# A spectral and MLP layer on one core: copies of x, an unread maximum and the written order of the first stage

## The chip, the cores and the metric

The kernel runs on one core of a Trainium2 chip. A time is the device time of one execution in microseconds (us). The core has a matrix engine (PE, with its weight loads PEld), a vector engine (DVE), an activation engine (ACT), a general engine (POOL) and SyncE (SP), which issues most transfers. Each engine works through its own instructions in the order in which they were written, and waits for another engine only where a semaphore says so. A transfer (DMA) runs beside the engines once it is issued. SBUF is the memory on the chip (the kernel's one large buffer there is called `arena`), PSUM holds the results of matmuls, and DRAM is the memory behind both.

## The reference

x has 2048 rows (tokens) of 576 numbers. It is normalised along each row to xn, and three things are added:

```
xn = (x - mean(x)) / sqrt(var(x) + 1e-5)
A  = Cr @ (xn @ Dr.T) - Ci @ (xn @ Di.T)     # Cr, Ci: 2048 x 2048; Dr, Di: 576 x 576
B  = relu(xn @ w1) @ w2                      # w1: 576 x 4608, w2: 4608 x 576
out = x + A + B
```

## The kernel before

**Number format.** The inputs are float32. Each operand of a matmul is written as a sum of two float16 numbers, a high part (made by ACT) and a low part (what is left, made by DVE or POOL), and a product takes three matmuls: high by high, high by low, low by high. Large products are formed from seven products of quarter blocks instead of eight, with sums and differences of the blocks formed by DVE.

**Stages.** Tokens are taken in 16 tiles of 128 rows, and four tiles make a group of 512. The columns of w1 are taken in 9 blocks. A step (block, group) computes a part of xn @ w1 and relu, and the second matmul of the step before. Sums of the second layer are collected in a DRAM buffer `spill`, which starts as a copy of x (`copy_x`) and to which every step adds by an accumulating transfer that POOL issues (`mlp2_out`, L665). Behind the steps come xn times the two small transform matrices, and then the product with the 2048 x 2048 matrices, which makes most of the rest.

**The first stage** covers about the first 80 us: the normalisation of all tiles and block 0 for the groups 0 to 2. Its order is written out by hand as a list of some 380 items; `pinned` runs them one by one and ties each instruction behind the one written before it on the same engine (PE, ACT, DVE, POOL, SP), so the list fixes the order on every engine. It fixes nothing between two engines; there only data and buffers decide. The items are:

- `counts`, `moments`, `stats`: mean, variance and factor of a tile or of a group of tiles (DVE, L271 to L299; the first step of `stats` is a square root on ACT, L289).
- `normal`, `high_x`, `low_x`, `again`: xn in float32, its high part, the low part in two pieces (piece 0 has 64 columns, piece 1 has 512), and a copy of the last 128 columns. The engine (V for DVE, A for ACT, GP for POOL) is an argument.
- `transposes` and `copies`: a tile is transposed by PE and copied out of PSUM by ACT (tiles 0 to 3). `transposes_dma` (L336): the same by a transfer that SP issues (tiles 4 to 15).
- `max_w1`, `sum_w2`, `steps_of`: scale factors of the weights; `steps_of` takes one small step, in turns on PE and DVE. `hi1`, `lo1`, `hi2`, `lo2`, `diff2`: the weights' parts and differences.
- `fill n`: n matmuls on zeros whose result nobody reads (PE, L914).
- `tile_by` (one tile) and `products` (a group of 512 rows): xn @ w1 on PE (L380). `outputs`: relu and the parts of its result (ACT and DVE, L431 to L441).
- `mlp2_mm` (PE, L643) and `mlp2_out` (ACT L658 or DVE L662, and POOL L665): the second layer, seven products, their evictions and the transfers that add to `spill`.
- `library` (L928): the maximum over partitions of a constant, on POOL, which nobody reads. It is the first instruction of that kind on POOL; the next ones scale block 1's weights (L168).
- `copy_x g` (L879): four transfers from x in DRAM to the four parts of `spill` for group g, 288 KB each, issued by SP.
- `work`: the next step of the preparation of block 1 (its loads L154 and L142, maxima L162, and the split of its weights, L232 on ACT and L235 on DVE).

Four staging buffers hold the normalised tiles; tile t uses buffer t % 4, so tile 12 takes the buffer that tile 8 had, once its transpose has landed. Block 1's split weights are written to the same memory, so the split waits for the transposes of tiles 12 to 14. The first matmuls of group 3 (the first thing behind the list) need the transposes of tiles 12 to 15.

The loads stand ahead of the list: on SP, the 16 tiles of x, the weights w1 of block 0 between the first tiles, and w2 behind tile 7.

```
def copy_x(g):
    for row, col in itertools.product(range(2), range(2)):
        ...
        with behind("td"):
            nc.sync.dma_start(spill[g, row, col], src.rearrange("(c p) e -> p c e", p=P))
```

`behind("td")` ties the copy behind the last `transposes_dma` written so far, if there is one.

Of the kernel before, what the change touches and what calls it, by code (L numbers as in the profile page):

```python
# [32 lines left out]
KM = 4  # L33
# [22 lines left out]
def kernel(  # L56
# [894 lines left out]
    for f, *a in (  # L951
        (counts, 0),
        (moments, 0),
        (stats, 0),
        (max_w1, 0, 0),
        (stats, 0),
        (fill, 50),
        (fill, 25),
        (stats, 0),
        (stats, 0),  # L960
        (stats, 0),
        (stats, 0),
        (max_w1, 0, 1),
        (steps_of, wa),
        (counts, 1),
        (high_x, 0),
        (normal, 0, A),
        (steps_of, wa),
        (fill, 4),
        (moments, 1),  # L970
        (stats, 1),
        (counts, 2),
        (stats, 1),
        (transposes, 0, *H),
        (fill, 10),
        (steps_of, wa),
        (steps_of, wa),
        (low_x, 0, 0, V),
        (copies, 0, 0, KM),
        (stats, 1),  # L980
        (steps_of, wa),
        (moments, 2),
        (hi1, 0),
        (stats, 1),
        (low_x, 0, 1, GP),
        (fill, 4),
        (steps_of, wa),
        (fill, 11),
        (transposes, 0, KM, NKX),
        (stats, 1),  # L990
        (stats, 1),
        (max_w1, 0, 2),
        (counts, 3),
        (high_x, 1),
        (moments, 3),
        (normal, 1, A),
        (max_w1, 0, 3),
        (stats, 2),
        (stats, 2),
        (counts, 5),  # L1000
        (stats, 2),
        (fill, 3),
        (low_x, 1, 0, V),
        (hi1, 1),
        (fill, 9),
        (tile_by, 0, (0,), XH[0], True, False),
        (stats, 2),
        (fill, 31),
        (low_x, 1, 1, GP),
        (transposes, 0, *L[1:-1]),  # L1010
        (transposes, 1, *H),
        (fill, 7),
        (transposes, 1, *L[1:-1]),
        (transposes, 1, KM, NKX),
        (copies, 0, KM, NKX + 1),
        (fill, 11),
        (copies, 1, 0, KM),
        (lo1, 0),
        (stats, 2),
        (stats, 2),  # L1020
        (tile_by, 0, (0,), XL, False, False),
        (copies, 1, KM, NKX + 1),
        (steps_of, wb),
        (lo1, 1),
        (steps_of, wb),
        (fill, 9),
        (tile_by, 0, (0,), XH[1], False, True),
        (normal, 2, V),
        (high_x, 2),
        (steps_of, wb),  # L1030
        (steps_of, wb),
        (tile_by, 0, (1,)),
        (low_x, 2, 0, V),
        (steps_of, wb),
        (counts, 4),
        (tile_by, 1, (0, 1), XH[0] + XH[1], True, False),
        (high_x, 3),
        (low_x, 2, 1, GP),
        (normal, 3, V),
        (low_x, 3, 1, GP),  # L1040
        (counts, 6),
        (sum_w2, 0, 0),
        (hi1, 2),
        (transposes, 2, *H),
        (moments, 5),
        (transposes, 2, *L[1:-1]),
        (counts, 7),
        (moments, 6),
        (moments, 4),
        (moments, 7),  # L1050
        (transposes, 2, KM, NKX),
        (copies, 2, 0, NKX + 1),
        (transposes, 3, *H),
        (tile_by, 1, (0, 1), XL, False, True),
        (low_x, 3, 0, GP),
        (lo1, 2),
        (transposes, 3, *L[1:-1]),
        (transposes, 3, KM, NKX),
        (tile_by, 2, (1,)),
        (tile_by, 2, (0,)),  # L1060
        (hi1, 3),
        (stats, 4),
        (stats, 4),
        (tile_by, 0, (2,)),
        (stats, 4),
        (stats, 4),
        (stats, 4),
        (stats, 4),
        (copies, 3, 0, NKX + 1),
        (lo1, 3),  # L1070
        (tile_by, 3, (0,)),
        (high_x, 4),
        (again, 4, GP),
        (tile_by, 2, (2,)),
        (normal, 4, V),
        (counts, 8),
        (normal, 5, A),
        (tile_by, 2, (3,)),
        (counts, 9),
        (counts, 11),  # L1080
        (outputs, 0, 0, "r"),
        (high_x, 5),
        (high_x, 6),
        (moments, 11),
        (tile_by, 1, (2,)),
        (moments, 9),
        (sum_w2, 0, 1),
        (normal, 6, V),
        (counts, 10),
        (tile_by, 3, (1,)),  # L1090
        (normal, 7, A),
        (tile_by, 3, (2,)),
        (steps_of, wb),
        (steps_of, wc),
        (moments, 10),
        (low_x, 4, 0, GP),
        (moments, 8),
        (low_x, 4, 1, GP),
        (stats, 8),
        (counts, 14),  # L1100
        (low_x, 5, 1, GP),
        (outputs, 0, 0, "hA"),
        (tile_by, 0, (3,)),
        (steps_of, wc),
        (stats, 8),
        (high_x, 7),
        (outputs, 0, 0, "hB"),
        (transposes_dma, 4),
        (low_x, 5, 0, GP),
        (low_x, 6, 0, GP),  # L1110
        (again, 6, GP),
        (tile_by, 1, (3,)),
        (stats, 8),
        (stats, 8),
        (again, 7, A),
        (again, 5, GP),
        (stats, 8),
        (stats, 8),
        (low_x, 6, 1, GP),
        (counts, 15),  # L1120
        (normal, 8, V),
        (high_x, 8),
        (normal, 10, A),
        (low_x, 7, 0, GP),
        (steps_of, wc),
        (tile_by, 3, (3,)),
        (transposes_dma, 5),
        (outputs, 0, 0, "s3"),
        (tile_by, 4, (0, 1)),
        (steps_of, wc),  # L1130
        (steps_of, wc),
        (tile_by, 5, (0, 1)),
        (outputs, 0, 1, "r"),
# [3 lines left out]
        (low_x, 7, 1, GP),  # L1137
        (outputs, 0, 0, "lA"),
        (low_x, 8, 0, V),
        (steps_of, wc),  # L1140
        (high_x, 9),
        (again, 8, A),
        (low_x, 8, 1, GP),
        (outputs, 0, 1, "s3"),
        (counts, 13),
        (transposes_dma, 6),
        (outputs, 0, 1, "s2"),
        (steps_of, wc),
        (low_x, 9, 1, GP),
        (high_x, 10),  # L1150
        (outputs, 0, 0, "s2"),
        (transposes_dma, 7),
        (high_x, 11),
        (outputs, 0, 1, "s1"),
        (steps_of, wc),
        (tile_by, 6, (0, 1)),
        (normal, 11, A),
        (tile_by, 7, (0, 1)),
        (outputs, 0, 1, "s4"),
        (outputs, 0, 0, "s4"),  # L1160
        (again, 9, GP),
        (again, 10, A),
        (low_x, 10, 1, GP),
        (outputs, 0, 1, "hA"),
        (steps_of, wc),
        (products, 1, 2),
        (outputs, 0, 1, "hB"),
        (outputs, 0, 0, "lB"),
        (hi2, 0, 0),
        (low_x, 9, 0, V),  # L1170
        (outputs, 0, 0, "s1"),
        (outputs, 0, 1, "lA"),
        (hi2, 1, 0),
        (products, 1, 3),
        (counts, 12),
        (lo2, 0, 0),
        (moments, 15),
        (lo2, 1, 0),
        (outputs, 1, 0, "r"),
        (outputs, 0, 0, "hS"),  # L1180
        (diff2, 0),
        (diff2, 1),
        (outputs, 0, 0, "lS"),
        (outputs, 1, 0, "s3"),
        (low_x, 10, 0, GP),
        (transposes_dma, 8),
        (diff2, 2),
        (low_x, 11, 0, GP),
        (outputs, 1, 0, "hB"),
        (hi2, 0, 1),  # L1190
        (moments, 14),
        (mlp2_mm, 0, 0, 0),
        (outputs, 1, 0, "s2"),
        (outputs, 0, 1, "hS"),
        (outputs, 1, 0, "hA"),
        (diff2, 3),
        (moments, 12),
        (transposes_dma, 9),
        (outputs, 1, 0, "lA"),
        (moments, 13),  # L1200
        (again, 11, GP),
        (outputs, 0, 1, "lB"),
        (hi2, 0, 2),
        (stats, 12),
        (transposes_dma, 10),
        (lo2, 0, 2),
        (low_x, 11, 1, GP),
        (outputs, 1, 0, "lB"),
# [6 lines left out]
        (outputs, 1, 0, "s1"),  # L1215
        (hi2, 1, 2),
        (mlp2_out, 0, 0, 0),
        (outputs, 0, 1, "lS"),
        (stats, 12),
        (outputs, 1, 1, "r"),  # L1220
        (lo2, 1, 2),
        (copy_x, 1),
        (hi2, 1, 1),
        (outputs, 1, 1, "hB"),
        (outputs, 1, 0, "hS"),
        (mlp2_mm, 0, 0, 1),
        (stats, 12),
        (mlp2_mm, 0, 0, 2),
        (outputs, 2, 0, "r"),
        (mlp2_out, 0, 0, 1),  # L1230
        (library,),
        (lo2, 1, 1),
        (mlp2_out, 0, 0, 2),
        (outputs, 1, 0, "lS"),
        (outputs, 1, 1, "s1"),
        (outputs, 2, 0, "s3"),
        (work, 0),
        (stats, 12),
        (mlp2_mm, 0, 0, 3),
        (stats, 12),  # L1240
        (mlp2_out, 0, 0, 3),
        (mlp2_mm, 0, 0, 4),
        (stats, 12),
        (normal, 14, A),
        (mlp2_out, 0, 0, 4),
        (outputs, 1, 1, "hA"),
        (outputs, 1, 1, "s3"),
        (mlp2_mm, 0, 0, 5),
        (work, 0),
        (outputs, 1, 1, "s2"),  # L1250
        (mlp2_mm, 0, 0, 6),
        (high_x, 15),
        (outputs, 1, 1, "s4"),
        (outputs, 1, 1, "lA"),
        (outputs, 2, 0, "s2"),
        (high_x, 13),
        (products, 2, 2),
        (high_x, 14),
        (work, 0),
        (mlp2_out, 0, 0, 5),  # L1260
        (outputs, 2, 0, "s1"),
        (normal, 15, A),
        (outputs, 1, 1, "lB"),
        (outputs, 2, 0, "hA"),
        (mlp2_out, 0, 0, 6),
        (outputs, 1, 1, "hS"),
        (again, 15, A),
        (again, 14, A),
        (outputs, 2, 0, "s4"),
        (mlp2_mm, 0, 1, 0),  # L1270
        (low_x, 15, 0, V),
        (high_x, 12),
        (mlp2_mm, 0, 1, 1),
        (normal, 12, V),
        (mlp2_out, 0, 1, 0),
        (products, 2, 3),
        (normal, 13, A),
        (outputs, 1, 1, "lS"),
        (low_x, 15, 1, V),
        (work, 0),  # L1280
        (mlp2_mm, 0, 1, 2),
        (low_x, 14, 0, V),
# [658 lines left out]
```

## Time and profile before

| | us |
|---|---|
| median of 3 runs | 1221.6 |
| lowest, highest | 1218.69, 1224.0 |
| the profiled execution | 1222.13 |
| its span, first to last instruction | 1220.4 |
| PE busy in the span | 1210.1 |
| DVE busy | 1007.9 |
| ACT busy | 724.4 |
| POOL busy | 161.0 |

Times inside the trace count from the span's first instruction. A row of a timeline gives the start, the time taken, engine, line, operation, what is written <- what is read, the shape and the number of instructions merged into it; in square brackets stands the idle time of the engine before it and what ended that. A row of the waits gives the waiting engine and line, what it waited for, the us in total, how often, and the longest.

### The profile page before, as it was taken

How to read it: one execution, taken by the hardware profiler on the slowest of the kernel's cores; microseconds unless marked ns; L12 is line 12 of the kernel's file. 1: busy time of each engine (PE TensorE's matmuls, PEld its weight loads, DVE VectorE, ACT ScalarE, POOL GpSimd, SP SyncE). 2: the span in 40 equal slices, each digit the busy share in tenths (PEclk: the TensorE clock that was granted, in tenths of full speed). 3: DMA queues.
4: the chain of work that ended last, by engine and by line, in shares of the span. 5: the costliest groups of instructions: out<-in, count | busy, mean ns of one | idle time of the engine just before them, and what ended most of it. 6: DMA issues, size and time to landing. Idle time of an engine off the chain costs nothing.

```text
span 1220.4 us, 24658 instructions
## 1 busy us (share of the span) xinstructions
PE 1210.1 (99%) x10233; PEld 958.5 (79%) x10233; DVE 1007.9 (83%) x1642; ACT 724.4 (59%) x1082; POOL 161.0 (13%) x199
## 2 busy tenths in 40 slices
PE   9989999999999999999999999999999999999998
PEld 8656567888888888888888888877777777777776
DVE  9988999887797788788877977678898978787875
ACT  7755565876676766757767766555644433433332
POOL 3231211111121211111121211100000000000000
PEclk9999999999999999999999999999999999999999
DMA  7895554867667675667576676520165254534320
GB/s 259 197 189 127 99 96 107 168 135 164 155 128 169 131 185 128 136 156 156 127 172 159 120 166 155 98 31 1 62 215 169 72 185 138 177 109 146 101 89 20
DMA packets 84064, 164.66 MB, mean 135 GB/s; under 512 B 22640, under 2 KB 43632, under 8 KB 83952
## 3 DMA queue, kind: packets, MB, share of 16 engines
q1 hardware_dynamic: 61168, 120.61, 31.1%
q0 software_dynamic: 22784, 42.48, 24.7%
q8 instruction: 80, 1.31, 0.4%
q14 instruction: 32, 0.26, 0.1%
HBM read 110.76 MB, written 53.08 MB: 134 GB/s over the span
## 4 chain that ended last, share of the span: by engine, by line
PE 94%; DMA 2%; DVE 2%; ACT 1%; issue 0%; SPq 0%; DVEq 0%; ACTq 0%
PE p L643 29%; PE p L1841 27%; PE bank L548 22%; PE p L380 7%; PE U L1630 4%; PE W L1630 2%; PE bank L567 1%; PE V L1630 1%; DMA arena<-in_x_dram 1%; DMA arena<-in_cim_dram 1%; DMA arena<-arena 1%; DVE arena L235 1%; DMA arena<-in_cre_dram 0%; ACT arena L232 0%; PE U L1646 0%
## 5 line engine op out<-in xcount | busy, mean ns | idle before, releaser
L643 PE MATMUL p<-arena 128*128 128x288 f16 x3024 | 398.6, 286 | 1.8 <-DVE arena L662 1.8
L643 PEld LDWEIGHTS <-arena 128*128 128x128 f16 x3024 | 295.9, 98 | 77.3 <-issue 2.2
L1841 PE MATMUL p<-arena 128*128 128x288 f16 x2688 | 329.4, 286 | 0.0
L1841 PEld LDWEIGHTS <-arena 128*128 128x128 f16 x2688 | 263.0, 98 | 66.3
L548 PE MATMUL bank<-arena 128*128 128x256 f16 x2580 | 304.8, 273 | 0.0
L548 PEld LDWEIGHTS <-arena 128*128 128x128 f16 x2580 | 250.2, 98 | 37.4 <-issue 5.9
L232 ACT ACTIVATE arena<-arena,sc_c 128x1024 f16<-128x1024 f32 x112 | 128.5, 1149 | 189.8 <-PE p L1841 137.8
L665 POOL DMA_DIRECT2D spill<-arena x144 | 128.7, 912 | 547.2 <-DVE arena L662 454.0
L235 DVE SCALAR_TENSOR_TENSOR arena<-arena,sc_c 128x1024 f16<-128x1024 f32 x112 | 143.3, 1280 | 29.4 <-ACT arena L232 26.4
L658 ACT ACTIVATE arena<-p,c_ub 128x576 f32<-128x576 f32 x144 | 105.9, 735 | 45.5 <-PE p L643 40.7
L235 DVE SCALAR_TENSOR_TENSOR arena<-arena,c_sw 128x640 f16<-128x640 f32 (+2 forms) x118 | 96.5, 848 | 32.5 <-ACT arena L232 30.6
L662 DVE SCALAR_TENSOR_TENSOR arena<-p,c_ub,arena 128x576 f32<-128x576 f32 x108 | 87.8, 813 | 22.2 <-PE p L643 19.6
L380 PE MATMUL p<-arena 128*128 128x128 f16 (+1 forms) x680 | 100.0, 303 | 3.1 <-issue 2.8
L576 DVE TENSOR_TENSOR arena<-bank,arena 128x512 f32<-128x512 f32 x84 | 57.7, 687 | 54.2 <-PE bank L548 53.2
L573 ACT ACTIVATE arena<-bank 128x512 f32<-128x512 f32 x112 | 66.5, 594 | 52.0 <-PE bank L548 51.9
L232 ACT ACTIVATE arena<-arena,c_sw 128x640 f16<-128x640 f32 (+2 forms) x118 | 89.3, 793 | 9.4 <-issue 4.5
L1630 PEld LDWEIGHTS <-arena 128*128 128x128 f16 x738 | 71.6, 98 | 19.7 <-issue 1.9
L380 PEld LDWEIGHTS <-arena 128*128 128x128 f16 x680 | 52.4, 98 | 43.3 <-issue 7.4
L579 ACT ACTIVATE arena<-arena 128x512 f16<-128x512 f32 x84 | 52.9, 630 | 52.5 <-DVE arena L576 51.6
L1849 DVE SCALAR_TENSOR_TENSOR arena<-p,us_c,arena 128x288 f32<-128x288 f32 x112 | 57.4, 513 | 27.0 <-PE p L1841 26.6
L1491 ACT ACTIVATE arena<-arena 128x1024 f32<-128x1024 f32 x64 | 67.0, 1047 | 7.6 <-DMA arena<-in_cim_dram 6.0
L589 DVE TENSOR_TENSOR arena<-arena 128x1024 f16<-128x1024 f32 x56 | 68.1, 1217 | 0.3 <-ACT arena L585 0.3
(134 smaller groups left out, 1050.4 us busy)
## 6 DMA issues: line engine op xcount, KB each, us to landing
spill<-arena POOLq DMA_DIRECT2D x144, 288.0 KB, 5.1
arena<-in_cre_dram SPq DMA_DIRECT2D x64, 512.0 KB, 4.6
arena<-in_cim_dram SPq DMA_DIRECT2D x64, 512.0 KB, 4.8
arena<-in_w_dram SPq DMA_DIRECT2D x17, 640.0 KB, 5.8
arena<-in_w_dram SPq DMA_DIRECT2D x18, 576.0 KB, 4.0
arena<-spill SPq DMA_DIRECT2D x40, 144.0 KB, 2.2
arena<-in_x_dram SPq DMA_DIRECT2D x16, 288.0 KB, 7.0
spill<-in_x_dram SPq DMA_DIRECT2D x16, 288.0 KB, 6.9
```

The lines of the kernel that those rows point to most:

```text
L232: nc.scalar.activation(hi, src, AF.Copy, scale=s)
L235: nc.vector.scalar_tensor_tensor(lo, src, s, hi, ALU.mult, ALU.subtract)
L380: order["m1"] = nc.tensor.matmul(ps[:, cols], w1s[b, i // 2][:, hl, i % 2 * KT + k], xT[g][:, kx, cols], start=(start and n == 0), stop=(s ...
L548: nc.tensor.matmul(ps[:, i], l, r, start=first and i == m == 0, stop=m == len(todo) - 1, skip_group_check=not first or i > 0,)
L589: order["lo"] = nc.vector.tensor_tensor(lo, stage[:, 1 + 2 * i :][:, :2], hi, ALU.subtract).ins
L643: order["pe"] = nc.tensor.matmul(ps[:, c], h[:, x, qa, c * P : (c + 1) * P], w[:, y, qb], start=first and i == 0 and j == 0, stop=i == NQ ...
L658: freed(nc.scalar.activation(o, ps, AF.Copy, scale=us[b]))
L662: add = nc.vector.scalar_tensor_tensor(o, ps, us[b], o, ALU.mult, ALU.add)
L665: nc.gpsimd.dma_start(spill[g, row, col], o, accum_op=ALU.add)
L1491: nc.scalar.activation(f, f, AF.Abs, scale=2.0**-10, accum_out=sums_c[:, n, q : q + 1])
L1630: nc.tensor.matmul(ps, l, r, start=first and m == 0, stop=m == len(todo) - 1, skip_group_check=not first,)
L1841: nc.tensor.matmul(ps, w[:, a, k], r[:, c, RQ[rq]], start=first and k == 0 and j == 0, stop=k == HK - 1 and j == 2, skip_group_check=not f ...
```

## The change

The list of items is written in another order. Three things in it are placed on purpose, and the rest of the list is arranged anew around them:

- `copy_x 0` becomes the first item of the list and `copy_x 1` follows some 45 items later; as SP has nothing between, their eight transfers stand on SP directly behind the loads of x. Before, they stood behind the transpose of tile 11.
- `copy_x 2` and `copy_x 3` stand behind the transpose of tile 11. Before, they stood behind the transpose of tile 15.
- `library` stands directly behind the transpose of tile 11, where POOL has not yet issued a transfer to `spill`. Before, it stood behind the first of these transfers.

The list holds the same items in the same number. Eleven of them change their engine: `low_x` 4 piece 0 and both pieces of `low_x` 10 go from POOL to DVE, `low_x` 8 and 9 piece 0 from DVE to POOL, `again` 4 and 6 from POOL to ACT, `again` 8 from ACT to POOL, `normal` 6 and 12 from DVE to ACT, `normal` 7 from ACT to DVE. Nothing outside the list is changed. The diff, cut to the parts that are spoken of:

```
     for f, *a in (
+        (copy_x, 0),
         (counts, 0),
         (moments, 0),
         (stats, 0),
-        (max_w1, 0, 0),
-        (stats, 0),
         (fill, 50),
-        (fill, 25),
         (stats, 0),
         (stats, 0),
         (stats, 0),
+        (max_w1, 0, 0),
         (stats, 0),
+        (stats, 0),
+        (high_x, 0),
         (max_w1, 0, 1),
+        (fill, 25),
+        (fill, 4),
+        (counts, 1),
         (steps_of, wa),
-        (counts, 1),
...
+        (transposes, 0, *H),
         (normal, 0, A),
-        (steps_of, wa),
-        (fill, 4),
         (moments, 1),
-        (stats, 1),
+        (fill, 10),
         (counts, 2),
         (stats, 1),
-        (transposes, 0, *H),
-        (fill, 10),
+        (fill, 4),
+        (fill, 11),
+        (fill, 3),
         (steps_of, wa),
...
         (max_w1, 0, 2),
+        (high_x, 1),
+        (copy_x, 1),
         (counts, 3),
...
         (hi2, 0, 1),
-        (moments, 14),
-        (mlp2_mm, 0, 0, 0),
+        (transposes_dma, 11),
+        (library,),
+        (products, 2, 0),
+        (copy_x, 2),
+        (lo2, 0, 1),
+        (mlp2_out, 0, 0, 0),
+        (products, 2, 1),
+        (high_x, 15),
+        (hi2, 1, 1),
+        (high_x, 12),
+        (hi2, 0, 2),
...
+        (copy_x, 3),
...
-        (transposes_dma, 11),
-        (products, 2, 0),
-        (products, 2, 1),
-        (lo2, 0, 1),
-        (copy_x, 0),
...
-        (copy_x, 1),
...
-        (library,),
...
+        (transposes_dma, 12),
+        (again, 13, A),
...
+        (low_x, 15, 1, V),
+        (transposes_dma, 13),
...
+        (transposes_dma, 14),
         (low_x, 15, 0, V),
...
+        (transposes_dma, 15),
...
-        (transposes_dma, 15),
-        (outputs, 2, 0, "lA"),
-        (work, 0),
-        (copy_x, 2),
...
-        (copy_x, 3),
```

More of the change, by code (lines that the diff above doesn't have):

```diff
@@ L1031 @@
+        (low_x, 2, 1, GP),
+        (high_x, 3),
+        (counts, 7),
         (steps_of, wb),
@@ L1088 @@
[L1088 to L1102, printed above, removed]
+        (normal, 4, V),
+        (counts, 11),
+        (high_x, 4),
+        (counts, 10),
+        (low_x, 4, 0, V),
```

488 lines of the change are left out of this document (243 added, 245 removed).

## The prediction

> **What bounds the kernel now.** I read the page's head first, then the waits of PE in the first 200 us, then two windows. The columns of a window are: stretch, its length, busy time and count of PE, weight loads, DVE, ACT and POOL, granted clock, DMA share, GB/s.
>
> ```profile
> span 1220.4 us, 24658 instructions
> PE 1210.1 (99%) x10233; PEld 958.5 (79%) x10233; DVE 1007.9 (83%) x1642; ACT 724.4 (59%) x1082; POOL 161.0 (13%) x199
> ...
> PE p L380 <- issue: 2.8, 1, 2.8
> PE p L643 <- DVE arena L662: 1.6, 1, 1.6
> ...
> PE pt L345 <- DVE arena L322: 0.4, 2, 0.2
> PE p L380 <- DMA arena<-arena: 0.2, 1, 0.2
> ...
> 70.00:80.00 10.00, 8.43 (x70) 6.61 (x68) 7.05 (x16) 6.30 (x9) 3.35 (x4) 1.00 1.23 184
> 80.00:90.00 10.00, 7.24 (x32) 2.84 (x31) 9.68 (x17) 2.75 (x4) 2.62 (x3) 0.83 1.15 279
> ```
>
> PE is busy for 1210.1 of 1220.4 us. The change leaves the list of PE's work as it is: the items are the same ones (the dummy matmuls of `fill` too), in another order. So the time can move only by PE's idle time, 10.3 us in all, and by its clock. Nearly half of the idle time stands in two gaps between 70 and 90 us, where the mean clock of one window is 0.83.
>
> ```profile
> 68.37 11.65 SPq L336 DMA_TRANSPOSE arena<-arena  x4
> 76.18 0.88 DVE L235 SCALAR_TENSOR_TENSOR arena<-arena,c_sw 128x640 f16<-128x640 f32 x1 [1.90 <-DMA arena<-arena]
> 76.98 0.81 DVE L662 SCALAR_TENSOR_TENSOR arena<-p,c_ub,arena 128x576 f32<-128x576 f32 x1
> 77.84 3.10 PE L643 MATMUL p<-arena 128*128 128x288 f16 x24 [1.57 <-DVE arena L662]
> 83.70 4.41 PE L380 MATMUL p<-arena 128*128 128x512 f16 x13 [2.76 <-issue]
> 88.58 2.98 PE L380 MATMUL p<-arena 128*128 128x512 f16 x13
> ```
>
> In this timeline the four transposes by DMA of tiles 12 to 15 are issued from 68.37 us. The weight split on DVE (L235) writes the staging buffer that tile 12's transpose reads, so it waits for that landing. The eviction L662 is queued behind it on DVE, and PE waits 1.57 us for L662. The second gap, 2.76 us, is filed under "issue"; line L336 (the transposes) names what it is. Its answer for 76 to 80 us, then 68 to 72, then 25 to 42:
>
> ```profile
>   PEld L380: 3.0, 1
> ...
> DMA to landing us min/median/max: 5.5/6.2/6.9
> ...
> L336 SPq DMA_TRANSPOSE arena<-arena x2: 3218/3382/3547, 68.4 to 72.0; - x2
> ...
> DMA to landing us min/median/max: 5.2/6.5/7.7
> ...
> L336 SPq DMA_TRANSPOSE arena<-arena x8: 1319/1375/1480, 25.4 to 40.0; - x8
> ...
> DMA to landing us min/median/max: 3.0/3.5/4.7
> ```
>
> The weight load of L380 waits for the last transpose, issued at 76.75 (80.02 less 3.27) and landed 6.9 us later, at 83.6. After that gap the 13 matmuls take 4.41 us where the same 13 take 2.98 at 88.58: 1.43 us more at the low clock. The place costs 1.57 + 2.76 + 1.43 = 5.8 us. Tiles 12 to 15 are transposed slowly (3.2 to 3.5 us to issue, 7.7 to land, against 1.4 and 3.5 for tiles 4 to 11), and POOL's rows say what runs beside them:
>
> ```profile
> 53.84 1.40 POOL L665 DMA_DIRECT2D spill<-arena  x1 [15.07 <-DMA arena<-in_w_dram]
> 62.82 1.30 POOL L928 PARTITION_ALL_REDUCE none<-eps  x1 [7.58 <-issue]
> 64.01 4.63 POOL L665 DMA_DIRECT2D spill<-arena  x4
> ...
> 74.57 1.09 POOL L665 DMA_DIRECT2D spill<-arena  x1 [2.70 <-DVE arena L662]
> 78.09 2.18 POOL L665 DMA_DIRECT2D spill<-arena  x2 [2.43 <-DVE arena L662]
> ```
>
> The unread maximum (L928) keeps POOL from 55.2 to 64.1 us, 8.9 us; the accumulating transfers behind it leave in a bunch of four from 64.0 to 68.6, and the transposes follow them.
>
> **The change part by part.** *The maximum* moves to just behind tile 11's transfer. On POOL it then follows the last copy of the tiles 8 to 11, which I put at 41 us below; with its 8.9 us it is done at 50, before the first accumulating transfer at 53.8. Cost nothing: what hides it is POOL's idle time of 15.07 us. Without that cover the accumulating transfers would come late as now. The bunch of four goes, each transfer leaving with its eviction.
>
> *Copies of groups 2 and 3.* Their eight issues on SP leave the place behind tile 15's transpose and go behind tile 11's, where groups 0 and 1 are copied now:
>
> ```profile
> L137 SPq DMA_DIRECT2D arena<-in_x_dram x16: 327/328/993, 0.7 to 17.6; - x16
> ...
> L879 SPq DMA_DIRECT2D spill<-in_x_dram x8: 597/616/1520, 41.5 to 46.2; - x8
> ...
> DMA to landing us min/median/max: 3.4/6.2/6.6
> ```
>
> The same eight transfers are there today, so nothing is added. What is queued behind them on SP, the loads of block 1, stays behind them.
>
> *Copies of groups 0 and 1* go behind the loads of x on SP, ahead of tile 4's transpose: 8 x 0.616 = 4.9 us of issue. The last load of x is issued at 17.6 us (L137), so the copies are issued by 22.5, or by 24 if SP holds each back for an earlier landing, as it does between the loads; tile 4's transpose, at 25.4 now (L336), is not held by the issue. Their data is another matter. If they land as far apart as today (last landing 46.2 + 6.6 = 52.8, first 41.5 + 3.4 = 44.9, so 7.9 us for the eight) they end near 30 us, and tile 4's transpose runs beside them.
>
> *The order.* Eleven items change their engine (POOL sheds some 1.5 us, ACT gains 1.1, DVE 0.1), which lies beside other work; where the items stand matters. The path from the first tiles to PE decides.
>
> ```profile
> 4.67 0.77 DVE L162 TENSOR_REDUCE c_mf<-arena 128x1 f32<-128x640 f32 x1
> ...
> 4.79 0.30 ACT L289 ACTIVATE s<-mv,eps 128x1 f32<-128x1 f32 x1 [2.57 <-DVE mv L276]
> ...
> 8.14 0.72 PE L914 MATMUL p<-idle 128*128 128x128 f16 x10
> ...
> 8.90 1.01 PE L914 MATMUL p<-idle 128*128 128x128 f16 x15
> ...
> 14.23 0.22 DVE L322 TENSOR_TENSOR arena<-arena 128x64 f16<-128x64 f32 x1
> 14.50 0.28 PE L345 MATMUL pt<-ident,arena 128*128 128x128 f16 x2 [0.17 <-DVE arena L322]
> ...
> 23.39 0.85 ACT L311 ACTIVATE arena<-arena,sh,r 128x576 f32<-128x576 f32 x1
> ...
> 28.78 3.30 PE L380 MATMUL p<-arena 128*128 128x128 f16 x56
> ...
> 29.42 0.16 DVE L299 SCALAR_TENSOR_TENSOR sh<-mv,r 128x4 f32<-128x4 f32 x1
> ...
> 31.38 1.16 POOL L322 TENSOR_TENSOR arena<-arena 128x512 f16<-128x512 f32 x1 [0.45 <-DMA arena<-arena]
> ...
> 34.01 9.33 PE L380 MATMUL p<-arena 128*128 128x128 f16 x84 [0.16 <-DMA arena<-arena]
> ...
> 44.65 6.48 PE L380 MATMUL p<-arena 128*128 128x512 f16 x28
> ```
>
> Tile 1: ahead of its low part on DVE (L322 at 14.23) stand the same kinds and numbers of operations as now, one step of the weights' scale fewer, and PE's work ahead of its transposes (14.50) is the same too. But two covers go. The square root of tile 0 on ACT (L289, until 5.09) now runs beside the maximum L162; with the maximum behind the steps of `stats`, DVE waits 0.4 for it. And the second small matmul of the weights' scale, now between 10 and 15 dummies, gets 18 more of these ahead (1.01 / 15 each, 1.2 us), so that DVE waits some 0.5 for it. The low part ends 0.9 later and PE, which has no slack there (0.17 idle), loses **0.9 us**. Bounds: 0, if DVE finds other work in these holes, and 1.7, the sum of both shifts in full.
>
> Tiles 4 to 7: PE starts them at 30.35 now (the last 28 of the 56 at 28.78), so at 31.3; the row at 34.01 shows it waiting 0.16 for tile 6's transpose already. I sum DVE's work ahead of tile 4's last step as 1 us more, so its transpose is issued near 26.5 and lands, by 3.0 to 4.7, at 29.5 to 31.2; tile 7's near 36, where PE arrives at 36.5. Beside the copies I add 0.5 us of landing that PE sees: **0.5**, nearest the rows of 25 to 42 us. Bounds: 0 (they land before PE comes) and 4.6 (tile 4 lands after 7.7, as tile 12 does, which is 2.9 behind PE, and tile 5, issued 2.0 later, costs 1.7 more).
>
> Tiles 8 to 11: ahead of the sixth step of their `stats` (L299, ends 29.58) DVE gets 2.9 us more: two tiles' `counts` 1.5, a `normal` traded for one of equal cost, the low part of tile 4 0.2, steps of w2's scale 0.7, an output 0.4, moments 0.2. With half of the waits above it ends near 32.9. ACT then does two `normal` and two `high_x` of 0.86 and a square root, until 36.6. POOL takes 0.6 for a copy and tile 8's small low part, so tile 8's transpose is issued at 37.3 and tile 11's, three issues of 1.4 on, at 41.5 (POOL's three small parts, two of 1.16 and a copy are done at 40.4); it is issued at 40.0 now. With 3.5 to land it is there at 45.0, where PE wants it at 44.65 + 0.9 + 0.5 = 46.0. Cost 0; the cover is 1 us, and a landing of 4.7 would use it up.
>
> Tiles 12 to 15: their low parts are written 10 us earlier on DVE; the last stands behind the eviction of `mlp2_mm` 0,1,1, so tile 15's transpose is issued near 70, and even with 3.5 to issue and 7.7 to land it is there by 78, where PE comes at 80.6. Tile 12's landing holds no eviction then. Both gaps go.
>
> Sum: -5.8 + 0.9 + 0.5 = -4.4; for the thinner cover of DVE behind 85 us (busy 9.68 of 10 in the window quoted) I add 0.3, bounds 0 and 1.5: **-4.1 us**. The profiled execution took 1222.13 us (span 1220.4 and 1.7 around it) and would take 1218.0; the median, 1221.6, lies 0.5 below that execution and would become **1217.5**.
>
> [...]
>
> **The rivals.**
> *The copies hold up tiles 4 to 7.* For it: eight transfers end near 30 us and tile 4's transpose is issued at 26.5 on the same queue; transposes beside other transfers took twice as long. Against it: POOL's four accumulating transfers were there, not copies. It decides from 4.6 us of waiting on (5.8 - 0.9 - 0.3), low clock included. Price at the upper bound 4.6, with 1.4 for a low clock behind a gap of 2.9, and up to 2 more for tile 11: 1221.6 - 5.8 + 0.9 + 6.0 + 2.0 + 0.3 = 1225.0, from 1221.6 on. Slower than before.
> [...] No run here shows copies and transposes in one queue at once.
> *The last transposes stay late.* The accumulating transfers are only spread, and one or two still run beside tile 15's transpose (one or two were in flight, POOL's rows at 74.57 and 78.09, when it took 6.9 us, with the bunch gone). Against it: 10 us of lead. Then the second gap stays and the first goes: 1221.6 - 1.6 + 1.7 = 1221.7.
> *No early loss.* DVE's holes fill, PE loses nothing early: 1221.6 - 5.8 = 1215.8, with a smaller start 1215.
> *The order starves PE in several places*, each over 2 us with the low clock behind it (4.2 us a time, as in the second gap): three such make 1221.6 - 4.1 + 12.6 = 1230.1. For it: DVE is busy 83% of the span, so every item written too early delays others; against it: PE has few waits now with a DVE as busy.
>
> **How the numbers follow.** Forecast 0.55 (1216 to 1219.5), no early loss 0.14 (1215 to 1216), strict clock rule 0.04 (1218.9), last transposes late 0.08 (1221.7), copies 0.12 (1221.6 to 1225), starved 0.07 (1228 up). The three runs lie within 0.2% of their middle, so a measured median may move by 2 us; half a per cent is 6.1 us, about what a measurement can tell. The range 1214.8 to 1223.0 leaves out the starved case, half of the copies and a little below. Faster needs 1215.5: half of the case without early loss (0.07) and, by a lucky median, a seventh of the forecast (0.08), so 0.15. Slower needs 1227.7: the starved case and a sixth of the copies, 0.09. Within: 0.76.
>
> **What would show it.** Right: PE's waits without the rows of 2.8 and 1.6, the clock 1.00 in 80 to 90 us, L336's landings near 4 us, L928 before 51 us, the transfers of L665 single. The early loss: a wait of L345 for L322 of about 1 us near 15. Wrong: a wait of L380 for DMA between 31 and 46 us, a clock below 1.00 anywhere before 90, or waits of L643 for DVE behind 85 us.

## The result and the profile after

The changed kernel takes 1218.05 us (median of 20 runs, 1216.92 to 1220.25); the kernel before, run beside it, 1221.8 (20 runs, 1217.74 to 1224.87). The ratio is 0.9975, with a 95% interval of 0.9965 to 0.9985: about 3 us faster (the two medians differ by 3.75), and within half a per cent. The profiled execution took 1217.57 us where that of before took 1222.13, so 4.56 less.

The head of the page after, then the waits of PE in the first 200 us, then the two windows from 70 to 90 us:

```profile
span 1215.8 us, 24650 instructions
...
PE 1208.5 (99%) x10233; PEld 959.2 (79%) x10233; DVE 1008.2 (83%) x1642; ACT 724.7 (60%) x1084; POOL 158.7 (13%) x197
```
```profile
...
PE p L380 <- DMA arena<-arena: 0.9, 1, 0.9
PE pt L345 <- ACT arena L350: 0.7, 1, 0.7
PE p L643 <- DVE arena L439: 0.6, 1, 0.6
PE pt L345 <- POOL arena L322: 0.5, 1, 0.5
```
```profile
70.00:80.00 10.00, 10.00 (x76) 7.24 (x75) 8.44 (x20) 4.05 (x8) 4.33 (x5) 1.00 1.09 209
80.00:90.00 10.00, 10.00 (x63) 5.59 (x61) 8.09 (x11) 4.62 (x9) 1.43 (x2) 1.00 0.99 203
```

PE is busy for all of both windows, at the full clock (1.00): the waits of 2.8 and 1.6 us are gone, and the slow 13 matmuls with them (2.97 us at 80.96, below). In their place stand four shorter waits, all before 55 us. The timeline of PE shows where:

```profile
14.51 0.40 PE L345 MATMUL pt<-ident,arena 128*128 128x128 f16 x4 [0.55 <-POOL arena L322]
15.60 0.27 PE L345 MATMUL pt<-ident,arena 128*128 128x128 f16 x2 [0.69 <-ACT arena L350]
...
35.40 9.33 PE L380 MATMUL p<-arena 128*128 128x128 f16 x84 [0.90 <-DMA arena<-arena]
...
52.86 8.99 PE L643 MATMUL p<-arena 128*128 128x288 f16 x72 [0.61 <-DVE arena L439]
...
80.96 2.97 PE L380 MATMUL p<-arena 128*128 128x512 f16 x13
```

And the timeline of POOL, with the rows of line L336 (the transposes by DMA of tiles 12 to 15):

```profile
45.83 0.42 POOL L928 PARTITION_ALL_REDUCE none<-eps  x1 [5.86 <-issue]
55.71 1.40 POOL L665 DMA_DIRECT2D spill<-arena  x1 [9.47 <-DVE arena L662]
60.17 1.09 POOL L665 DMA_DIRECT2D spill<-arena  x1 [3.06 <-DVE arena L662]
63.18 1.08 POOL L665 DMA_DIRECT2D spill<-arena  x1 [1.92 <-DVE arena L662]
```
```profile
L336 SPq DMA_TRANSPOSE arena<-arena x4: 1325/1554/1882, 59.9 to 70.6; - x4
...
DMA to landing us min/median/max: 4.5/5.3/6.8
```

The maximum (L928) lies in POOL's idle time, the accumulating transfers (L665) leave one by one, and the last transpose is issued at 70.6 us, 10 us before PE needs it at 80.96 (the first matmuls of group 3).

PE executes the same 10233 matmuls in both kernels, so one can compare when the n-th of them starts. Matmul 790, in the mlp2 row at 72.14, starts 1.9 us later than before (75.69 against 73.78). Behind the place, at 95 us, PE is 4.2 us ahead, and stays so up to 316 us; behind a small wait at 331 us that of these two only the kernel before has, it is 4.6 ahead, to the end. So the place gave 1.9 + 4.2 = 6.1 us, and the first 75 us took 1.9 of it back.

### The profile page after: what moved, and what is told of

Read it like the earlier page. It is cut to its first block, busy times and chain, and to the rows that moved or that the text cites. A ratio compares the mean times of both kernels' runs of the same rounds, so it can differ in the third digit from the quotient of the medians.

```text
span 1215.8 us, 24650 instructions
## 1 busy us (share of the span) xinstructions
PE 1208.5 (99%) x10233; PEld 959.2 (79%) x10233; DVE 1008.2 (83%) x1642; ACT 724.7 (60%) x1084; POOL 158.7 (13%) x197
## 4 chain that ended last, share of the span: by engine, by line
PE 96%; DVE 3%; ACT 1%; issue 0%; POOL 0%; DVEq 0%
PE p L643 30%; PE p L1841 27%; PE bank L548 23%; PE p L380 5%; PE U L1630 4%; PE W L1630 2%; PE bank L567 1%; PE V L1630 1%; DVE st L271 1%; PE p L914 1%; DVE arena L235 0%; PE U L1646 0%; PE p L405 0%; DVE arena L313 0%; ACT arena L317 0%; ACT arena L232 0%
## 5 line engine op out<-in xcount | busy, mean ns | idle before, releaser
L665 POOL DMA_DIRECT2D spill<-arena x144 | 128.4, 895 | 546.3 <-DVE arena L662 475.1
L380 PE MATMUL p<-arena 128*128 128x128 f16 (+1 forms) x680 | 97.9, 300 | 0.9 <-DMA arena<-arena 0.9
L380 PEld LDWEIGHTS <-arena 128*128 128x128 f16 x680 | 52.1, 98 | 39.1 <-issue 3.1
```

Source lines behind the costliest of these rows:

```text
L380: order["m1"] = nc.tensor.matmul(ps[:, cols], w1s[b, i // 2][:, hl, i % 2 * KT + k], xT[g][:, kx, cols], start=(start and n == 0), stop=(s ...
L665: nc.gpsimd.dma_start(spill[g, row, col], o, accum_op=ALU.add)
```

## The experiments

**Theory.** The move of the maximum takes the two gaps away. The new order costs something early and gives nothing that the move does not give. The copies matter little. **Rivals.** The new order is what takes the gaps away; or the copies of groups 0 and 1 are what makes PE wait for tile 6 at 35 us.

The change has three parts that can be undone singly: the maximum's place, the places of the four copies, and the order (with its changes of engine). All eight combinations were run. The medians, with the ratio to runs of the kernel before on the same chip:

| maximum | copies | order | median us (runs) | ratio, 95% interval |
|---|---|---|---|---|
| old | old | old | 1221.8 (20) | 1 |
| **new** | old | old | 1216.21 (6) | 0.9953 (0.9937 to 0.9968) |
| old | **new** | old | 1222.36 (12) | 1.0005 (0.9991 to 1.0019) |
| old | old | **new** | 1220.38 (12) | 0.9987 (0.9975 to 0.9998) |
| **new** | **new** | old | 1216.74 (5) | 0.9960 (0.9946 to 0.9973) |
| **new** | old | **new** | 1217.21 (10) | 0.9964 (0.9951 to 0.9977) |
| old | **new** | **new** | 1219.57 (12) | 0.9986 (0.9974 to 0.9997) |
| **new** | **new** | **new** | 1218.05 (20) | 0.9975 (0.9965 to 0.9985) |

**The maximum alone.** The kernel before, with one line moved:

```
         (transposes_dma, 11),
+        (library,),
         (products, 2, 0),
...
         (mlp2_out, 0, 0, 1),
-        (library,),
         (lo2, 1, 1),
```

> The kernel before with one edit: the unread maximum stands directly behind tile 11's transpose; the rest of the list is as before. If the bunch of four accumulating transfers is the cause of the late transposes, each transfer leaves with its eviction (from 53.8, 58.2, 60.9, 62 and 67 us), the transposes of tiles 12 to 15 still start at 68.4 but take about 1.5 to 2 us each to issue, tile 15's lands by 79.5 where PE comes at 79.4, both gaps go and, with no early loss, the time is 1221.8 - 5.8 = 1216.0 (up to 1217.5 if a short wait for tile 15 is left). If the order of the low parts is what counts, the transposes stay late by the second gap and the time is 1219 to 1222. If the copies count, 1221.8.

Measured: 1216.21 us, ratio 0.9953 [0.9937, 0.9968]; PE is 6.1 us ahead of the kernel before at 97 us. Its waits of PE up to 200 us, POOL's timeline, and the rows of line L336 for tiles 12 to 15:

```profile
...
PE p L380 <- DMA arena<-arena: 0.5, 1, 0.5
PE pm L204 <- DVE mb L683: 0.3, 1, 0.3
PE p L380 <- issue: 0.2, 1, 0.2
```
```profile
44.61 0.38 POOL L928 PARTITION_ALL_REDUCE none<-eps  x1 [6.25 <-DMA spill<-in_x_dram]
53.44 1.40 POOL L665 DMA_DIRECT2D spill<-arena  x1 [8.45 <-DVE arena L662]
```
```profile
L336 SPq DMA_TRANSPOSE arena<-arena x4: 1397/1446/2745, 68.0 to 73.8; - x4
...
DMA to landing us min/median/max: 3.2/4.1/5.2
```

It follows that one moved line, without any other part of the change, takes both gaps away, and that this kernel beats both the one before and the changed one: its highest time (1217.18) lies below all but three of the changed kernel's twenty.

**The copies alone.** The kernel before, with copies 0 and 1 at the head of the list, and 2 and 3 behind tile 11's transpose:

```
     for f, *a in (
+        (copy_x, 0),
+        (copy_x, 1),
         (counts, 0),
...
         (transposes_dma, 11),
+        (copy_x, 2),
+        (copy_x, 3),
```

(Here and below, the code cuts show the new places of what is moved, and not every line at an old place.)

> The kernel before with one edit: copies of x for groups 0 and 1 behind the loads of x, for groups 2 and 3 behind tile 11's transpose. If the bunch behind the unread maximum is the cause, both gaps stay and the time is within 1.5 us of 1221.8; PE may also wait for the transposes of tiles 4 to 7 beside the copies, by up to 1 us more than the 0.16 of before. If the copies' place made the gain, 1217 to 1218.

Measured: 1222.36 us, ratio 1.0005 [0.9991, 1.0019]. The waits of PE:

```profile
PE p L380 <- issue: 2.4, 1, 2.4
PE p L643 <- DVE arena L662: 1.7, 1, 1.7
PE p L380 <- DMA arena<-arena: 1.1, 2, 0.9
```

Both gaps stay. The wait for tile 6's transpose near 35 us grows from 0.2 to 0.9, and one of 0.2 comes at 30.5 us. By themselves the copies gain nothing.

**The change with the maximum put back**, to behind `(mlp2_out, 0, 0, 1)`:

```
         (transposes_dma, 11),
-        (library,),
...
         (mlp2_out, 0, 0, 1),
+        (library,),
```

> The changed kernel with one edit undone: the unread maximum stands behind the first accumulating transfer again. The transfers leave in a bunch near 66 us and the transposes of tiles 13 to 15, issued from 64 to 71 us, take 3.2 to 3.5 us to issue and up to 7.7 to land again. If the new order's lead of some 10 us is enough by itself, PE still meets no gap: 1218 to 1219. If the bunch alone decides, tile 15 lands at 82 or later, 1 us or more behind PE, with a low clock behind it: 1219.5 to 1222.

Measured: 1219.57 us, ratio 0.9986 [0.9974, 0.9997]. The gap at 80 us does not return (tile 15 lands at 79.9). Another wait does. The timelines of POOL, DVE and PE:

```profile
64.98 0.38 POOL L928 PARTITION_ALL_REDUCE none<-eps  x1 [7.80 <-issue]
65.25 2.42 POOL L665 DMA_DIRECT2D spill<-arena  x2
66.67 1.34 POOL L168 PARTITION_ALL_REDUCE top<-c_mw  x1
```
```profile
68.05 0.15 DVE L171 TENSOR_SCALAR half<-top 128x1 f32<-128x1 f32 x1 [2.05 <-POOL top L168]
```
```profile
70.24 1.03 PE L643 MATMUL p<-arena 128*128 128x288 f16 x7 [1.74 <-DVE arena L441]
```

The useful maximum L168 is queued on POOL behind the unread one, DVE waits for it, and PE for what DVE does next. So the new order takes the old gaps away too, but makes the late maximum costly in another way. The time lies in the range that was expected if the bunch alone decides, but not for that reason: neither of the two expected ways had this wait.

**The change with the copies put back** to where they stood (0 and 1 behind tile 11's transpose, 2 and 3 behind tile 15's):

```
-        (copy_x, 0),
         (counts, 0),
...
-        (copy_x, 1),
...
         (transposes_dma, 11),
+        (copy_x, 0),
+        (copy_x, 1),
         (library,),
...
         (transposes_dma, 15),
+        (copy_x, 2),
+        (copy_x, 3),
```

> The changed kernel with one edit undone: copies for groups 0 and 1 behind tile 11's transpose, for groups 2 and 3 behind tile 15's, as before. If the copies beside tiles 4 to 7 cost what I predicted (0.5 us), PE's wait of 0.90 us for tile 6 shrinks to some 0.4 and the time is 1217.5. If that wait comes from the order of the low parts alone, it stays at 0.9 and the time at 1218.0. If the copies' place made the gain, 1221.

Measured: 1217.21 us, ratio 0.9964 [0.9951, 0.9977]. Tile 4 lands at 29.1 instead of 30.8, but PE waits 0.9 for tile 6 all the same, and stands 4.1 us ahead of the kernel before at 100 us, as in the changed kernel (4.2). (The median lies 0.8 us below the 1218.0 that was expected in this case; the intervals of the two kernels overlap.) In the new order the wait at 35 us is the order's, not the copies'.

**All three moves in the old order**, the edits of the first two experiments together:

```
     for f, *a in (
+        (copy_x, 0),
+        (copy_x, 1),
         (counts, 0),
...
         (transposes_dma, 11),
+        (library,),
+        (copy_x, 2),
+        (copy_x, 3),
```

> The kernel before with the three placed moves alone (the unread maximum and the eight copies 2 and 3 behind tile 11's transpose, copies 0 and 1 behind the loads of x) in the old order of everything else. If the effects add up, the maximum gains 5.5 us (1216.2 was measured alone) and the copies beside tiles 4 to 7 cost PE some 0.9 us, as in the trace of the run with the copies alone: 1217.0, with 0.9 us of waits for the transposes of tiles 4 to 6. Then the searched order costs about 1 us net (1218.05 measured). If the searched order helps once the moves are made, this is slower than 1218.0.

Measured: 1216.74 us, ratio 0.9960 [0.9946, 0.9973]; the only wait of PE of over 0.2 us from 2 to 200 us is one of 0.8 for tile 6. The new order on top of the same moves makes it 1218.05: it costs some 1.3 us by the medians and 1.0 by the traces (PE 5.6 us ahead to the end here, 4.6 there).

**The order alone:** the changed kernel with the maximum and the copies both put back.

```
-        (copy_x, 0),
         (counts, 0),
...
         (transposes_dma, 11),
-        (library,),
+        (copy_x, 0),
+        (copy_x, 1),
...
         (mlp2_out, 0, 0, 1),
+        (library,),
...
         (transposes_dma, 15),
+        (copy_x, 2),
+        (copy_x, 3),
```

> The new order and the engines it gives to eleven items, with the maximum and all four copies where they stood before. Theory (the maximum's place decides; the new order costs a little by itself and takes some of the bunch apart; the copies cost nothing in it): the time stays at that of the new order with the maximum put back, 1219.6, so 1219.0 to 1220.0; PE waits again for DVE's L441 near 70 us, by 1.5 to 2 us; tile 6's transpose holds PE 0.8 to 1.0 us near 34 us though no copy is near. Rival (the new place of the copies is what keeps the last transposes clear of the accumulating transfers): a wait of over 2 us of L380 near 80 us and a low clock come back, 1221 to 1223.

Measured: 1220.38 us, ratio 0.9987 [0.9975, 0.9998]. The waits of PE:

```profile
PE p L643 <- DVE arena L441: 1.9, 1, 1.9
PE pt L345 <- POOL arena L322: 1.1, 1, 1.1
PE p L643 <- DVE arena L439: 1.1, 1, 1.1
```

Here too the old gaps are gone with the bunch of transfers still late, so the copies' new places are not what takes them away. The wait behind the late maximum stands in their place. Two things came otherwise than expected: the time lies 0.4 us above the expected range, and tile 6's transpose does not hold PE. PE comes to it later than in the changed kernel, behind waits of 1.12 and 0.77 us near 15 us and a stretch of low clock (0.50) from 16.1 to 19.5 us (its rows are in the last section).

**Copies 0 and 1 alone, and copies 2 and 3 alone**, each in the old order with the maximum moved; the edits are the two halves of that of the copies, but copies 2 and 3 stand directly behind those of groups 0 and 1.

```
     for f, *a in (
+        (copy_x, 0),
+        (copy_x, 1),
         (counts, 0),
...
         (transposes_dma, 11),
+        (library,),
```
```
         (transposes_dma, 11),
+        (library,),
...
         (copy_x, 1),
+        (copy_x, 2),
+        (copy_x, 3),
```

> The old order with the maximum moved and only the copies of groups 0 and 1 moved behind the loads of x. Theory (these copies land beside tiles 4 to 7 and cost 0.9 us there in the old order): L380 waits 0.8 to 0.9 us for tile 6's transpose near 34 us, PE stands 5.2 us ahead of the kernel before behind 97 us (6.1 without the copies), 1216.7 to 1217.1. Rival (the copies behind tile 11 are what cost the 0.9 us): L380 waits 0.5 as with the maximum moved alone, PE 6.1 us ahead, 1216.2.

> The old order with the maximum moved and only the copies of groups 2 and 3 moved, to behind those of groups 0 and 1, all eight behind tile 11's transpose. Theory (copies 2 and 3 cost nothing): as with the maximum moved alone, PE 6.1 us ahead behind 97 us, 1216.2, within 0.4. Rival (they hold up the loads of block 1 or the four last transposes): a new wait of L380 near 80 us or of the weight split, 1217 or more.

Measured: 1216.93 us, ratio 0.9954 [0.9940, 0.9969], and 1216.94, ratio 0.9952 [0.9937, 0.9968]. The medians do not tell them apart. The traces do; PE's row of tiles 6 and 7 in the first and in the second:

```profile
34.84 9.33 PE L380 MATMUL p<-arena 128*128 128x128 f16 x84 [0.86 <-DMA arena<-arena]
```
```profile
33.81 9.33 PE L380 MATMUL p<-arena 128*128 128x128 f16 x84 [0.22 <-DMA arena<-arena]
```

At 100 us PE is 5.3 us ahead of the kernel before with copies 0 and 1 moved, and 6.4 with 2 and 3 moved. In the old order this wait is 0.78 to 0.90 us in the three traces with copies 0 and 1 behind the loads of x, and 0.16 to 0.51 in the four without: these copies cost PE some 0.3 to 0.7 us there. Copies 2 and 3 cost nothing that the trace shows; the median is 0.3 us above the range expected for that (1216.2, within 0.4), but none of the rival's waits is there.

**No unread maximum.** The kernel before without the item `library`; only a result that nobody reads is left out.

```
         (mlp2_out, 0, 0, 1),
-        (library,),
         (lo2, 1, 1),
```

> The kernel before without the unread maximum; the result it would have is read by nobody, so nothing else is left out. Theory (the first maximum over partitions on POOL costs 6 to 8 us of that engine whichever one it is, and the useful one, L168, is first now): L168 stands at 66 us or later with 5 to 8 us of idle time in front of it, DVE's L171 waits for it and PE behind DVE, at least 1.5 us; accumulating transfers behind L168 come in a bunch; 1218 to 1222. Rival (the idle time belongs to the place at 55 to 63 us and not to the first such instruction): L168 starts with under 1 us of idle in front, no bunch, no gap, 1216.2 as with the maximum moved.

Measured: 1219.39 us, ratio 0.9975 [0.9963, 0.9987]: 2.4 us less than with the maximum at its old place, 3.2 more than with it moved. POOL, DVE, PE, and the rows of line L336 for tiles 12 to 15:

```profile
67.52 1.08 POOL L665 DMA_DIRECT2D spill<-arena  x1 [4.08 <-DVE arena L662]
75.47 0.38 POOL L168 PARTITION_ALL_REDUCE top<-c_mw  x1 [6.86 <-issue]
```
```profile
75.88 0.15 DVE L171 TENSOR_SCALAR half<-top 128x1 f32<-128x1 f32 x1 [3.75 <-POOL top L168]
```
```profile
77.39 6.24 PE L643 MATMUL p<-arena 128*128 128x288 f16 x36 [2.20 <-DVE arena L662]
```
```profile
L336 SPq DMA_TRANSPOSE arena<-arena x4: 1408/1441/2692, 68.8 to 74.5; - x4
```

The bunch that was expected behind L168 did not come: the next three transfers start at 77.64, 79.16 and 81.10 us, one by one. In both kernels it is POOL's first maximum over partitions that has the idle time in front of it: 7.58 us ahead of L928 before, 6.86 ahead of L168 here. Where the unread one has run, L168 starts with no idle time ahead of it once its data is there (at 63.91 us in the changed kernel, at 66.67 with the maximum put back). The unread one takes that time early, and that is its use; where it stands decides whom it keeps waiting.

**Mending the early waits of the changed kernel.** Three small edits: the copies of tile 1's second half behind its last transposes; the second small matmul of the weights' scale back behind 10 dummies; both together with output `s4` of group 1 ahead of `again 15`.

```
         (transposes, 1, *L[1:-1]),
-        (copies, 1, 0, KM),
         (transposes, 1, KM, NKX),
+        (copies, 1, 0, KM),
```
```
         (fill, 10),
+        (steps_of, wa),
         (counts, 2),
...
         (fill, 3),
-        (steps_of, wa),
         (low_x, 0, 1, GP),
```
```
         (outputs, 1, 0, "s2"),
+        (outputs, 1, 0, "s4"),
         (again, 15, A),
...
         (lo2, 0, 2),
-        (outputs, 1, 0, "s4"),
```

> The changed kernel with one pair exchanged: the last two transposes of tile 1 stand ahead of the copy of its first four columns, as in the kernel before. If PE's 0.69 us at 15 us comes from that copy on ACT, the wait goes (at most 0.2 left for the low part on DVE) and the time is 1217.5. If it comes from DVE's lateness, as I predicted, it stays and the time is 1218.0.

> The changed kernel with one item moved: the second small matmul of the weights' scale stands behind 10 dummies instead of 28, as in the kernel before. If its lateness reaches PE by way of the weight split, the normalisation of tile 1 on ACT and its low part on POOL, the wait of 0.55 us for POOL near 14 us shrinks to 0.1 or less, and the time is 1217.5. If it is harmless, 1218.0.

> The changed kernel with both of these edits and a third: the fourth sum of group 1 is written ahead of a weight part that waits for ACT, so that DVE frees the PSUM bank earlier. If PE's early loss of 1.6 us is the three waits near 14, 15 and 53 us and the one for tile 6, the first three go (0.55, 0.69, 0.61), the last may grow by what PE is early (up to 1.2 us, since tile 6 does not come sooner): 1216.2 to 1217.4. If the waits only move on to the next item, 1218.

Measured: 1217.55 us, ratio 0.9968 [0.9956, 0.9979]; 1217.62, ratio 0.9964 [0.9952, 0.9977]; 1217.21, ratio 0.9967 [0.9951, 0.9982]. The intervals overlap with that of the changed kernel, so none is shown to be faster. With the first edit the wait of 0.69 is gone, a new one of 0.28 for the weight split follows, and PE stands 0.5 us further ahead at 100 us. With the second the wait for POOL is 0.41 instead of 0.55; with all three edits, the second among them, it is 0.59, so the 0.14 shows nothing. With all three, PE's waits up to 40 us:

```profile
14.08 0.69 PE L345 MATMUL pt<-ident,arena 128*128 128x128 f16 x6 [0.59 <-POOL arena L322]
...
31.40 3.30 PE L380 MATMUL p<-arena 128*128 128x128 f16 x56 [0.68 <-DMA arena<-arena]
35.76 9.33 PE L380 MATMUL p<-arena 128*128 128x128 f16 x84 [1.05 <-DMA arena<-arena]
```

The waits for ACT's copy and for DVE's L439 are gone, and the waits for the transposes by DMA are longer. (This profiled execution, 1219.13 us, has the highest time of its six, so its sizes need not be typical.) In this profile what was mended came back as another wait: the tiles' transposes are next.

## Why the prediction was right, and where it was not

The forecast was 1217.5 us, the median is 1218.05, and the profiled execution fell by 4.56 us where the sum says 4.1. Step by step:

- *The place at 70 to 90 us, 5.8 us.* Right, in place and kind: both gaps and the low clock are gone, and PE gained 6.1 us there. (Of the four transposes before that were called slow to issue, one was not: tile 14's took 1.42 us.)
- *The maximum costs nothing at its new place and unbunches the transfers.* Right: it ends at 46.3 us (the bound was 50), 9.5 us ahead of the first transfer. But the prediction did not ask what this step does alone. It put the end of the gaps down to the low parts written earlier ("tile 15's transpose is issued near 70"). The step holds (70.6, landed at 76.4), and was not needed: with the maximum alone moved, the last transposes are issued until 73.8, land by 79.0 and cost PE 0.2 us. One sign that was named did not come: the landings of L336 were to be near 4 us, and the median is 5.3.
- *Tile 1, 0.9 us.* The size was right, the cause wrong. The waits of L345 for tiles 0 and 1 are 0.4 in all before and 1.24 after, 0.84 more. The step named DVE's low part. That part ends 0.4 us later (14.85 against 14.45), not 0.9, and PE does not wait for it. The trace has POOL's low part (0.55) and ACT's copy (0.69): the new list puts `copies 1` ahead of the last transposes of tile 1, which go to the same PSUM buffer. The step weighed the order on DVE and not this buffer. The small matmul does come later, at 10.28 instead of 8.79 us. The wait of 0.4 for L204 also goes, but not by the new order: in that order it is 0.43 us with the maximum put back, 0.68 with the copies put back and 0.28 with all three edits. What sets its size no run shows.
- *Copies 0 and 1, 0.5 us.* The size was near (the wait for tile 6 grew from 0.2 to 0.9), the cause wrong in this kernel: the copies landed by 29.7 us, before tile 6's transpose was issued at 30.1, and the wait is there without them. It is the order's, which issues tile 6 0.9 us later. In the old order the copies do cost 0.3 to 0.7. A wait of L380 for DMA between 31 and 46 us was named as a sign of being wrong; it came (0.90 us), where the sum held 0.5 for it.
- *Copies 2 and 3 and tiles 8 to 11, nothing.* Right: tile 11 issued at 41.0 (forecast 41.5), landed at 44.4 (45.0), no wait.
- *Not in the sum:* 0.61 us at 52.86, where output `s4` of group 1 (L439) stands on DVE behind a weight's low part that waits 1.7 us for ACT, and PE waits for the PSUM bank which that output frees.
- *+0.3 behind 85 us.* It was -0.4: no wait came there, and one of 0.24 at 331 us went. The traces of these kernels differ there by up to 2 us with no edit near, so no such step of a few tenths can be told from one profile.

The early terms are near in sum (forecast 1.4; PE's idle time up to matmul 790 is 3.73 us after and 2.13 before, 1.6 more, and the matmul starts 1.9 later), but by two causes exchanged for others of the same size: that is luck. Tenths should not be read from one pair of profiles: at 30 us PE's lead already differs by 0.8 us among the four traces of the old order that have no edit ahead of it. The spread of the runs was put too low as well: the three runs before lay within 0.24%, not 0.2, and twenty spread over 7 us. Of the rivals, *the copies*, *the last transposes* and *the starved order* did not come; *no early loss* (1215 to 1216) is nearly what the move of the maximum alone gives, 1216.2.

*The 1218.9 in the list of chances* is 1217.5 with the 1.43 us of low clock kept. It lies close to the median, but no run shows that term: the low clock went with the gap (1.00 in both windows from 70 to 90 us), and the 13 matmuls that took 4.41 us take 2.97.

## What to carry to other kernels

Take a change of several parts apart before costing it: here one moved line of some 380 gives more than the whole change, and a new order for all the rest costs some 1 us of it. POOL's first maximum over partitions, with 5.9 to 7.9 us of idle time in front of it in these traces, belongs where POOL has nothing due, and what is queued behind it decides its price. Where a list is written anew, look for each PSUM buffer that two items share, not only for the order on each engine.

## What the runs showed of the hardware

**The granted clock.** Its mean over the span is 0.998 or 0.999 in four of the fourteen traces (the kernel before, the copies alone, the order alone, and no maximum) and 1.000 in the ten others. In each of the four one stretch of 3.4 us before the end reads 0.50: from 83.25 to 86.66 us, 85.24 to 88.65, 16.12 to 19.53 and 78.02 to 81.42. In stretches of that length, rows of PE's busy time and clock read as follows: the kernel before, the order alone, and no maximum.

```profile
76.42:79.83 3.41, 1.99 (x17) 1.59 (x17) 3.41 (x6) 2.08 (x3) 1.74 (x2) 1.00 1.19 176
79.83:83.25 3.42, 1.11 (x10) 0.66 (x7) 3.11 (x8) 0.29 (x1) 1.69 (x2) 1.00 1.30 208
83.25:86.66 3.41, 2.96 (x8) 1.03 (x9) 3.41 (x5) 1.88 (x3) 0.00 (x0) 0.50 1.07 269
```
```profile
12.70:16.11 3.41, 1.52 (x25) 1.27 (x22) 3.38 (x14) 3.08 (x6) 1.16 (x1) 1.00 1.03 417
16.12:19.53 3.41, 3.41 (x31) 2.92 (x31) 3.12 (x10) 3.12 (x4) 1.14 (x1) 0.50 1.04 405
...
70.73:74.14 3.41, 2.23 (x14) 1.35 (x15) 3.41 (x5) 1.62 (x4) 0.00 (x0) 1.00 1.19 170
74.14:77.55 3.41, 3.41 (x24) 2.12 (x23) 2.98 (x8) 0.38 (x2) 1.07 (x1) 1.00 1.31 191
```
```profile
74.60:78.01 3.41, 1.21 (x11) 0.82 (x10) 2.10 (x6) 1.75 (x3) 0.75 (x2) 1.00 0.96 185
78.02:81.42 3.40, 3.40 (x17) 2.17 (x15) 3.32 (x7) 2.79 (x5) 2.30 (x3) 0.50 0.95 233
```

In the stretch ahead of the low one PE idled 1.89 us (3.41 - 1.52, the order alone), 2.20 (no maximum), 2.31 (the kernel before) and 2.35 (the copies alone, busy 1.05 of 3.40 us from 81.83 to 85.23). Behind stretches with 1.42 us (3.41 - 1.99) and 1.18 (3.41 - 2.23) of idle time the clock stayed at 1.00. The length of a single gap does not tell which: the one of 1.88 us in the order alone (70.03 to 71.91) had 1.00 behind it, and the two waits of 1.12 and 0.77 us in the same trace had 0.50. What decides it these runs do not show. That low stretches are part of why the kernel before spreads over 7 us fits the granted clock on record for each run: of its 67 runs beside the experiments, the 14 with a mean clock of 0.997 took 1223.05 to 1226.26 us, and the 21 with 1.000 took 1218.11 to 1221.57. The ten kernels whose traces have no low clock before the end spread over 0.7 to 3.5 us, and 86 of their 88 runs have 0.999 or 1.000.

**The first maximum over partitions.** The rows MODIFY_POOL_CONFIG of line L928 (of L168 where L928 is left out) stand ahead of it on POOL; what POOL does between them and the maximum no row shows. The two times behind the durations are the first and the last start. They are, for the kernel after, before, and no maximum:

```profile
L928 POOLq MODIFY_POOL_CONFIG  x2: 14/14/14, 40.2 to 40.2; - x2
```
```profile
L928 POOLq MODIFY_POOL_CONFIG  x2: 517/520/522, 55.0 to 55.1; - x2
```
```profile
L168 POOLq MODIFY_POOL_CONFIG  x2: 537/540/542, 68.3 to 68.4; - x2
```

From there to the maximum's own row it takes 5.6 us (to 45.83) after, 7.8 (to 62.82) before and 7.1 (to 75.47) without it. It is 6.1 with the maximum alone moved, 8.0 with the maximum put back and 8.2 in the order alone. So it was 7.1 to 8.2 us in the four of these traces in which an accumulating transfer was issued just ahead, and 5.6 and 6.1 in the two others.

**Transposes beside accumulating transfers.** Tiles 12 to 15 took a median of 3.1 and 3.2 us to issue in the two traces in which four accumulating transfers left in a bunch just ahead of them (copies alone, and the kernel before), and 1.4 to 1.6 in eight others (the changed kernel, the maximum alone and put back, all three moves, the order alone, the two halves of the copies, and no maximum). That POOL is busy with its first maximum is not the cause: without the unread one it is so beside these transposes (68.3 to 75.5 us), and their median is 1.4. That the bunch is the cause fits, but no run changed the bunch alone.
